# Attention scores in separate buffers, logits written straight into a group's rows, state update moved, fills moved ahead

## The chip, the cores and the metric

The kernel runs on one core of one Trainium2 chip. The metric is the device time of one execution in microseconds (us); the value before is the median of three runs. The engines are called by the profile's names: PE (matrix multiply; PEld is its weight load), DVE (vector), ACT (scalar), POOL (GpSimd) and SP, whose queue issues most of the transfers.

## The reference

The input is a gated linear attention with batch 4, 8 heads, 768 steps and head size 48, then a mixture of experts with 8 experts on the 3072 resulting rows of 384 numbers. All is float32.

```python
for t in range(S):
    state = alpha[:, :, t, :, None] * state + k[t] (outer) v[t]
    y[:, :, t] = q[t] @ state
x = y.transpose(0, 2, 1, 3).reshape(B * S, H * D)
logits = normalised(x) @ normalised(expert_emb).T / tau
expert_idx = argmax(logits, axis=1)
for e in range(E):                      # each token goes to one expert
    h = maximum(x[mask] @ w1[e], 0.0)   # 384 -> 1024
    out[mask] = gate_w[mask, None] * (h @ w2[e])
```

## The kernel before

The first stage computes attention and routing, the second (from L705 on) the experts. The sequence is cut into chunks of 128 steps: 6 per batch, 24 in all. The loop at L640 runs over an iteration number s and is a software pipeline. Iteration s does, in the order of the program text: `load(s + 2)`; `keys_back(s - 1)`, which turns the scaled keys on PE and copies them (ACT, `kb`); `rows(s - 3)`; `decays(s)`, which turns alpha, keys and queries on PE, runs two scans on DVE (`r` L458, `a` L472) and scales keys (DVE, `kr`) and queries (ACT copy `qc`, POOL product `qs`, L477); `decay_state(s - 1)` (POOL); `scores(s - 1)`; `update(s - 1)`; `mix_states(s - 2)` and `mix_chunk(s - 2)`; then the routing steps. Every third iteration `choose(g)` picks experts for a group of chunks on DVE (L310 to L317), and the iteration after it `place(g)` computes the rows in `xs` to which `to_rows` sends the tokens by indirect transfers from POOL. GROUPS (L61) has ten groups: six of three chunks, two of two, two of one.

The steps around the change, in the order of a chunk's life:

- `scores` multiplies keys and queries into one accumulator tile `sc` with two halves (even and odd heads). DVE masks half 0 into half 0 of the tile `sm` (L541); ACT copies half 1 into half 1 of the same tile (L544), and POOL clears the part above the diagonal (L545). `sm` has two buffers, `sc` one.
- `update` multiplies kept keys and values into `pd` (16 matmuls, L517), and DVE adds the result to the decayed state (L527), which POOL decays in the next iteration (`dec`, L502).
- `mix_states` (16 matmuls, L565) and `mix_chunk` (16 matmuls, L578) fill the accumulator `pyx`, which has one buffer; ACT copies its first part to `yT` (L584).
- one iteration later `rows` multiplies `yT` with a selection matrix `sel` (8 matmuls, L594) into the rest of `pyx`. DVE sums the two halves of the logits (`lg`, L603), ACT copies them into the token's row `x` (L607), two more ACT copies (L609) bring the 384 numbers, and a POOL copy (L601) the token's number. `x` has six buffers, one chunk each.

The matrix `sel` and the padded expert matrix `embp` are filled by POOL in `prepare_logits` (L270, L278, L285, L286: two fills and eight copies), which is put behind the scaled queries of chunk 1 by `behind(1)`.

Each engine runs its own queue in order and waits on semaphores. The program is written for a framework that places the waits and whose planner sets the order within each queue: it follows the program text, but by its own estimate of when operands are ready, so that some steps are interleaved (the turns of alpha for the next chunk stand partly ahead of the matmuls of `rows`). `behind(s)` forces what is inside it behind DVE's scan `a` and POOL's product `qs` of chunk s on these queues.

Of the kernel before, what the change touches and what calls it, by code (L numbers as in the profile page):

```python
# [27 lines left out]
def kernel(  # L28
# [155 lines left out]
    with ExitStack() as c1:  # L184
# [20 lines left out]
        def fixed_parts():  # L205
# [21 lines left out]

        sel = keep.tile([P, 2, NP // 2, 2 * D + E], FP32, name="sel")
        group_of = [g for g, (a, b) in enumerate(GROUPS) for _ in range(a, b)]
        lg_g = [  # L230
            keep.tile([P, b - a, E], FP32, name=f"lg{g}") for g, (a, b) in enumerate(GROUPS)
        ]

        al0 = keep.tile([P, NP, NS], FP32, name="al0")

        emb = work.tile([E, DM], FP32, name="emb", bufs=1)

        def prepare_loads():
            a0 = work.tile([NS, H, DP], FP32, name="a0", bufs=1)
            nc.vector.memset(a0[:, :, D:DP], 1.0)  # L240
            for b in range(B):
                nc.scalar.dma_start(
                    out=a0[b * NCH : (b + 1) * NCH, :, 0:D], in_=a_r[b, :, 0]
                )
            nc.scalar.dma_start(out=emb, in_=expert_emb)
            nc.scalar.dma_start(out=rtau, in_=tau.to_broadcast([P, 1]))
            return a0
# [11 lines left out]
        def prepare_logits():  # L259

            nc.vector.reciprocal(rtau, rtau)
            e2 = work.tile([E, DM], FP32, name="e2", bufs=1)
            en = work.tile([E, 1], FP32, name="en", bufs=1)
            nc.scalar.activation(e2, emb, AF.Square, accum_out=en)
            nc.scalar.activation(en, en, AF.Sqrt)
            nc.vector.tensor_scalar(en, en, 1e-6, None, ALU.add)
            nc.vector.reciprocal(en, en)
            nc.vector.tensor_tensor(en, en, rtau[:E], ALU.mult)
            embp = work.tile([E, 2, NP // 2, 2, DP], FP32, name="embp", bufs=1)
            nc.gpsimd.memset(embp, 0.0)  # L270
            for hh in range(2):
                nc.vector.tensor_scalar(
                    embp[:, hh, :, :, 0:D],
                    emb.rearrange("e (q j a d) -> e a q j d", q=NP // 2, j=2, a=2)[:, hh],
                    en, None, ALU.mult,
                )
            pe = ps_tr.tile([P, 2, NP // 2, E], FP32, tag="tr", name="pe")
            nc.gpsimd.memset(sel, 0.0)  # L278
            for hh in range(2):
                for q in range(NP // 2):  # L280
                    nc.tensor.transpose(
                        pe[:, hh, q],
                        embp[:, hh, q].rearrange("e j d -> e (j d)"), ident[:E, :E],
                    )
                    nc.gpsimd.tensor_copy(sel[0:DP, hh, q, 0:D], ident[0:DP, 0:D])  # L285
                    nc.gpsimd.tensor_copy(  # L286
                        sel[DP:P, hh, q, D : 2 * D], ident[DP:P, DP : DP + D]
                    )
            nc.vector.tensor_copy(sel[:, :, :, 2 * D :], pe)

# [12 lines left out]
        def choose(g):  # L303

            s0, s1 = GROUPS[g]
            n = s1 - s0
            shp = [P, n, E]
            l = lg_g[g][:, 0:n]
            top = work.tile([P, GMAX], FP32, name="top")[:, 0:n]
            nc.vector.tensor_reduce(top.unsqueeze(2), l, axis=AX.X, op=ALU.max)  # L310
            win = work.tile([P, GMAX, E], FP32, name="win")[:, 0:n]
            nc.vector.tensor_tensor(win, l, bc(top, shp, 2), ALU.is_equal)
            nc.vector.tensor_tensor(win, win, bc(first, shp, 1), ALU.mult)
            best = work.tile([P, GMAX], FP32, name="best")[:, 0:n]
            nc.vector.tensor_reduce(best.unsqueeze(2), win, axis=AX.X, op=ALU.max)
            ch = chosen[:, s0:s1]
            nc.vector.tensor_tensor(ch, win, bc(best, shp, 2), ALU.is_equal)  # L317
            for s in range(s0, s1):
                eng = nc.vector if s == NS - 1 else nc.gpsimd
                eng.tensor_tensor(before[:, s + 1], before[:, s], chosen[:, s], ALU.add)  # L320
# [103 lines left out]
        def load(s):  # L424

            if s < NS:
                b, c = divmod(s, NCH)
                i = s % NBUF
                for p0, p1 in ((1, AROW), (AROW, P)):
                    nc.sync.dma_start(out=at_s[i][p0:p1, :, 0:D], in_=a_r[b, c, p0:p1])  # L430
                nc.sync.dma_start(out=kt_s[i][:, :, 0:D], in_=k_r[b, c])
                nc.sync.dma_start(out=qt_s[i][:, :, 0:D], in_=q_r[b, c])
            if s > 0:
                b, c = divmod(s - 1, NCH)
                nc.sync.dma_start(out=vt_s[(s - 1) % NBV][:, :, 0:D], in_=v_r[b, c])
# [93 lines left out]
        def scores(s):  # L529

            d = st[s]
            kr, qs = d["kr"], d["qs"]
            d["sm"] = sm = work.tile([P, 2, NP, P], FP32, name="sm")
            sc = ps_sc.tile([P, 2, NP, P], FP32, name="sc")
            for p in range(NP):
                for hh in range(2):
                    sl = slice(DP * hh, DP * hh + DP)
                    nc.tensor.matmul(  # L538
                        sc[:, hh, p], lhsT=kr[sl, p], rhs=qs[sl, p], start=True, stop=True
                    )  # L540
            nc.vector.tensor_tensor(  # L541
                sm[:, 0], sc[:, 0], causal.to_broadcast([P, NP, P]), ALU.mult
            )
            nc.scalar.copy(sm[:, 1], sc[:, 1])  # L544
            nc.gpsimd.affine_select(  # L545
                out=sm[:, 1], in_=sm[:, 1], pattern=[[0, NP], [1, P]], base=0,
                channel_multiplier=-1, compare_op=ALU.is_ge, fill=0.0,
            )

# [21 lines left out]
        def mix_chunk(s):  # L571

            d = st[s]
            pyx, sm, vt = d["pyx"], d["sm"], vt_s[s % NBV]
            for hh in range(2):
                for p in range(NP):
                    q, to = p // 2, DP * (p % 2)
                    nc.tensor.matmul(  # L578
                        pyx[to : to + DP, hh, q * P : (q + 1) * P],
                        lhsT=vt[:, 2 * p + hh], rhs=sm[:, hh, p],  # L580
                        start=("dec" not in d and q == 0), stop=True, skip_group_check=True,
                    )
            d["yT"] = yT = work.tile([P, 2, NQ, P], FP32, name="yT")
            nc.scalar.copy(yT.rearrange("p a q t -> p a (q t)"), pyx[:, :, 0:YX])  # L584

        def rows(s):

            yT = st[s]["yT"]
            px = st[s]["pyx"][:, :, YX : YX + NQ * (2 * D + E)].rearrange(
                "t a (q n) -> t a q n", q=NQ  # L590
            )
            for hh in range(2):
                for q in range(NQ):
                    nc.tensor.matmul(  # L594
                        px[:, hh, q], lhsT=yT[:, hh, q], rhs=sel[:, hh, q], start=True, stop=True,
                        skip_group_check=True,
                    )
            g = group_of[s]
            s0, s1 = GROUPS[g]
            st[s]["x"] = x = work.tile([P, ROW], FP32, name="x", bufs=6)  # L600
            nc.gpsimd.tensor_copy(x[:, TK : TK + 1], toks[:, s : s + 1])  # L601
            l = lg_g[g][:, s - s0]
            nc.vector.tensor_reduce(  # L603
                l.unsqueeze(2), px[:, :, :, 2 * D :].rearrange("t a q e -> t e a q"),
                axis=AX.XY, op=ALU.add,
            )
            nc.scalar.copy(x[:, LG : LG + E], l)  # L607
            for hh in range(2):
                nc.scalar.copy(  # L609
                    x[:, 0:DM].rearrange("t (q j a d) -> t a q j d", q=NQ, j=2, a=2)[:, hh],  # L610
                    px[:, hh, :, 0 : 2 * D].rearrange("t q (j d) -> t q j d", j=2),
                )

        exg = xg_s[NXG - 1]
        exT = work.tile([P, KT, EARLY * P], FP32, name="exT", bufs=1)
# [20 lines left out]
        fixed_parts()  # L636
        load(0)
        a0 = prepare_loads()
        load(1)
        for s in range(NS + 4):  # L640
            if s + 2 <= NS:
# [10 lines left out]
            if 0 <= s - 1 < NS:  # L652
                decay_state(s - 1)
                scores(s - 1)
                update(s - 1)
            if 0 <= s - 2 < NS:
                mix_states(s - 2)
                mix_chunk(s - 2)
            if s == 1:
                with behind(s):  # L660
# [22 lines left out]
                        first_expert()  # L683
            with behind(s) if s < NS else ExitStack():
                for c in send[:] if s >= S0 + 3 else send[:1]:
                    to_rows(dest[:, c : c + 1], st[c]["x"])
                    send.remove(c)
            if r == S0 - 1:
                fetch_early()
# [259 lines left out]
```

## Time and profile before

| | |
|---|---|
| time, median of 3 runs (lowest to highest) | 480.54 us (479.85 to 486.49) |
| profiled execution | 481.05 us, its span 479.3 us |
| mean granted PE clock, share of full speed | 0.994 |
| PE busy | 444.9 us, 93% of the span |
| DVE, ACT, POOL busy | 176.3, 150.3, 139.3 us |
| attention stage | to about 173 us; the experts' stage fills the rest |

The span goes from the first to the last instruction of the profiled execution. Busy shares are averages over two stages with different limits, so they are read by stretch. The chain that ended last covers only the final part of the span here, and is not used.

### The profile page before, as it was taken

The page shows a single profiled execution, that of the slowest core. Times are in us where ns is not written, and L with a number is a line of the kernel's source. Part 1 is how long each engine was busy: PE and PEld are TensorE (multiplying, and loading weights), DVE is VectorE, ACT ScalarE, POOL GpSimd, SP SyncE. Part 2 cuts the span into 40 slices and gives each one's busy share as a digit, 9 for nine tenths or more (in the row PEclk, how much of TensorE's full clock was granted, in tenths as well). Part 3 has the DMA queues.
Part 4 walks back from the last instruction along what each step waited for, and adds up shares of the span by engine and source line. Part 5 has one row for each costly group of instructions (what it writes and reads, how often), then busy time and mean ns, then how long its engine had stood idle before and what let it go on. Part 6 is the DMA issues. An engine that isn't in the chain of part 4 may idle for free. (4 is left out here: it accounts for less than half of the span.)

```text
span 479.3 us, 8450 instructions
## 1 busy us (share of the span) xinstructions
PE 444.9 (93%) x3124; PEld 315.1 (66%) x3125; DVE 176.3 (37%) x467; ACT 150.3 (31%) x352; POOL 139.3 (29%) x236
## 2 busy tenths in 40 slices
PE   5798979888897999999999999999999999999993
PEld 4587868778786788577555555557557555655551
DVE  6777575776858751441211111111211121111010
ACT  3234434334343443463530421202540250210200
POOL 4546655655654742610001011010200101002001
PEclk9999989999999999999999999999999999999998
DMA  9999976876871396395503606301800900001000
GB/s 143 158 165 159 182 143 130 138 155 127 168 133 53 108 356 235 105 327 185 209 18 115 239 18 220 125 34 25 306 30 16 326 6 35 15 0 46 1 16 31
DMA packets 119358, 59.96 MB, mean 125 GB/s; under 512 B 102287, under 2 KB 113816, under 8 KB 119312
## 3 DMA queue, kind: packets, MB, share of 16 engines
q1 hardware_dynamic: 115208, 49.14, 44.4%
q0 software_dynamic: 3728, 10.16, 5.9%
q8 instruction: 28, 0.46, 0.4%
q14 instruction: 18, 0.15, 0.1%
q10 hardware_dynamic: 376, 0.05, 0.1%
HBM read 49.69 MB, written 11.45 MB: 128 GB/s over the span
## 5 line engine op out<-in xcount | busy, mean ns | idle before, releaser
L783 PE MATMUL ph<-xT,w 128*128 128x384 f32 (+1 forms) x384 | 119.6, 462 | 1.7 <-ACT hT L787 0.7
L794 PE MATMUL pyo<-w,hT 128*128 128x384 f32 x352 | 115.6, 488 | 0.0
L783 PEld LDWEIGHTS ph<-xT,w 128*128 128x128 f32 x384 | 67.6, 190 | 44.6 <-issue 5.2
L794 PEld LDWEIGHTS pyo<-w,hT 128*128 128x128 f32 x352 | 66.3, 190 | 45.3
L721 POOL DMA_INDIRECT out_dram<-y,sx x25 | 24.2, 967 | 239.6 <-DVE y L797 169.5
L787 ACT ACTIVATE hT<-ph 128x384 f32<-128x384 f32 (+1 forms) x64 | 28.6, 460 | 114.2 <-PE ph L783 114.1
L797 DVE TENSOR_SCALAR y<-pyo,gt 128x384 f32<-128x384 f32 x22 | 13.6, 617 | 114.1 <-PE pyo L794 114.1
L594 PE MATMUL pyx<-sel,yT 128*128 128x104 f32 x192 | 26.7, 282 | 15.7 <-ACT yT L584 15.3
L477 POOL TENSOR_TENSOR qs<-qc,a 128x512 f32<-128x512 f32 x24 | 30.5, 1271 | 26.0 <-DVE a L472 16.0
L594 PEld LDWEIGHTS pyx<-sel,yT 128*128 128x128 f32 x192 | 23.3, 191 | 19.4 <-ACT yT L584 19.2
L544 ACT COPY sm<-sc 128x512 f32<-128x512 f32 x24 | 14.1, 587 | 61.1 <-DVE sm L541 61.1
L458 DVE TENSOR_TENSOR_SCAN r<-pa,inr 128x511 f32<-128x511 f32 x24 | 29.2, 1218 | 4.5 <-PE pa L414 4.1
L292 POOL DMA_INDIRECT xs<-x,dest x24 | 24.6, 1024 | 19.3 <-DVE dest L341 11.7
L472 DVE TENSOR_TENSOR_SCAN a<-pa,ini 128x512 f32<-128x512 f32 x24 | 29.4, 1223 | 0.9
L538 PE MATMUL sc<-qs,kr 64*128 64x128 f32 x384 | 29.6, 291 | 0.1
L578 PE MATMUL pyx<-sm,vt 128*64 128x128 f32 x384 | 26.3, 278 | 2.1 <-DVE sm L541 2.1
L538 PEld LDWEIGHTS sc<-qs,kr 64*128 64x128 f32 x384 | 24.6, 192 | 4.5 <-issue 2.9
L737 DVE COPY xT<-pxg 128x384 f32<-128x384 f32 (+1 forms) x30 | 14.7, 498 | 30.3 <-PE pxg L736 27.3
L578 PEld LDWEIGHTS pyx<-sm,vt 128*64 128x64 f32 x384 | 20.5, 136 | 5.6 <-issue 3.4
L414 PE MATMUL pa<-ident,at 128*128 128x128 f32 x96 | 18.3, 287 | 4.3 <-DMA at<-in_alpha_dram 4.3
L746 ACT ACTIVATE gx<-xg 128x384 f32<-128x384 f32 x32 | 16.7, 522 | 14.5 <-DMA xg<-xs 13.3
L476 ACT COPY qc<-pq 128x512 f32<-128x512 f32 x24 | 14.1, 586 | 11.5 <-PE pq L414 10.7
(168 smaller groups left out, 524.6 us busy)
## 6 DMA issues: line engine op xcount, KB each, us to landing
w<-in_moe_w_dram SPq DMA_DIRECT2D x16, 1536.0 KB, 8.0
kt<-in_k_dram SPq DMA_DIRECT2D x24, 192.0 KB, 3.9
qt<-in_q_dram SPq DMA_DIRECT2D x24, 192.0 KB, 4.5
vt<-in_v_dram SPq DMA_DIRECT2D x24, 192.0 KB, 4.0
xg<-xs SPq DMA_DIRECT2D x22, 196.5 KB, 7.6
at<-in_alpha_dram SPq DMA_DIRECT2D x24, 168.0 KB, 3.9
xg<-xs SPq DMA_DIRECT2D x8, 98.2 KB
at<-in_alpha_dram SPq DMA_DIRECT2D x24, 22.5 KB, 4.1
```

Source lines behind the costliest of these rows:

```text
L292: ins = nc.gpsimd.indirect_dma_start(out=xs, out_offset=bass.IndirectOffsetOnAxis(ap=rows, axis=0), in_=x, in_offset=None, bounds_check=E ...
L414: nc.tensor.transpose(pt[:, p * P : (p + 1) * P], t[:, 2 * p : 2 * p + 2].rearrange("p h d -> p (h d)"), ident,)
L458: nc.vector.tensor_tensor_scan(r[:, L - 2 :: -1], pa[:, L - 1 : 0 : -1], inr[:, L - 2 :: -1], 1.0, ALU.mult, ALU.add,)
L472: by_dve = nc.vector.tensor_tensor_scan(a, pa, ini, 0.0, ALU.mult, ALU.add)
L477: by_pool = nc.gpsimd.tensor_tensor(qs.rearrange("p n t -> p (n t)"), qc, a, ALU.mult)
L538: nc.tensor.matmul(sc[:, hh, p], lhsT=kr[sl, p], rhs=qs[sl, p], start=True, stop=True)
L578: nc.tensor.matmul(pyx[to : to + DP, hh, q * P : (q + 1) * P], lhsT=vt[:, 2 * p + hh], rhs=sm[:, hh, p], start=("dec" not in d and q == 0) ...
L594: nc.tensor.matmul(px[:, hh, q], lhsT=yT[:, hh, q], rhs=sel[:, hh, q], start=True, stop=True, skip_group_check=True,)
L721: ins = nc.gpsimd.indirect_dma_start(out=out, out_offset=bass.IndirectOffsetOnAxis(ap=col, axis=0), in_=y, in_offset=None, bounds_check=N - 1,
L783: nc.tensor.matmul(ph, lhsT=w1_t[:, i, f * P : (f + 1) * P], rhs=xT[:, i], start=(i == 0), stop=(i == KT - 1),)
L787: nc.scalar.activation(hT[:, f], ph, AF.Relu)
L794: nc.tensor.matmul(py, lhsT=hT[:, f], rhs=w2_t[:, f], start=(f == 0), stop=(f == FT - 1),)
```

## The change

The two halves of `sc` and of `sm` become two tiles each, of half the size. The logits are summed straight into the rows of a group's buffer `x` (one tile for up to three chunks, three buffers), out of which `choose` reads them and `to_rows` sends; the logits' own tiles `lg` and ACT's copy of them go away, ACT's two copies of the 384 numbers become one, and the token numbers are copied once per group and not once per chunk. `update` is called between `mix_states` and `mix_chunk`. The ten POOL fills for `embp` and `sel` are called ahead of `load(1)`, and so ahead of the queries of chunk 0.

```diff
+        def prepare_fills():
+            nc.gpsimd.memset(embp, 0.0)
+            nc.gpsimd.memset(sel, 0.0)
+            for hh in range(2):
+                for q in range(NP // 2):
+                    nc.gpsimd.tensor_copy(sel[0:DP, hh, q, 0:D], ident[0:DP, 0:D])
+                    nc.gpsimd.tensor_copy(
+                        sel[DP:P, hh, q, D : 2 * D], ident[DP:P, DP : DP + D]
+                    )
...
-            l = lg_g[g][:, 0:n]
+            l = x_g[g][:, :, LG : LG + E]
...
-            d["sm"] = sm = work.tile([P, 2, NP, P], FP32, name="sm")
-            sc = ps_sc.tile([P, 2, NP, P], FP32, name="sc")
+            d["sm"] = sm = [work.tile([P, NP, P], FP32, name=f"sm{hh}") for hh in range(2)]
+            sc = [ps_sc.tile([P, NP, P], FP32, name=f"sc{hh}") for hh in range(2)]
...
-            nc.vector.tensor_tensor(
-                sm[:, 0], sc[:, 0], causal.to_broadcast([P, NP, P]), ALU.mult
-            )
-            nc.scalar.copy(sm[:, 1], sc[:, 1])
+            nc.vector.tensor_tensor(sm[0], sc[0], causal.to_broadcast([P, NP, P]), ALU.mult)
+            nc.scalar.copy(sm[1], sc[1])
...
-            st[s]["x"] = x = work.tile([P, ROW], FP32, name="x", bufs=6)
-            nc.gpsimd.tensor_copy(x[:, TK : TK + 1], toks[:, s : s + 1])
-            l = lg_g[g][:, s - s0]
+            if s == s0:
+                x_g[g] = work.tile([P, GMAX, ROW], FP32, name="x", bufs=3)[:, 0 : s1 - s0]
+                nc.gpsimd.tensor_copy(x_g[g][:, :, TK], toks[:, s0:s1])
+            x = x_g[g][:, s - s0]
             nc.vector.tensor_reduce(
-                l.unsqueeze(2), px[:, :, :, 2 * D :].rearrange("t a q e -> t e a q"),
+                x[:, LG : LG + E].unsqueeze(2), px[:, :, :, 2 * D :].rearrange("t a q e -> t e a q"),
                 axis=AX.XY, op=ALU.add,
             )
-            nc.scalar.copy(x[:, LG : LG + E], l)
-            for hh in range(2):
-                nc.scalar.copy(
-                    x[:, 0:DM].rearrange("t (q j a d) -> t a q j d", q=NQ, j=2, a=2)[:, hh],
-                    px[:, hh, :, 0 : 2 * D].rearrange("t q (j d) -> t q j d", j=2),
-                )
+            nc.scalar.copy(
+                x[:, 0:DM].rearrange("t (q j a d) -> t a q j d", q=NQ, j=2, a=2),
+                px[:, :, :, 0 : 2 * D].rearrange("t a q (j d) -> t a q j d", j=2),
+            )
...
         a0 = prepare_loads()
+        prepare_fills()
         load(1)
...
                 scores(s - 1)
+            if 0 <= s - 2 < NS:
+                mix_states(s - 2)
+            if 0 <= s - 1 < NS:
                 update(s - 1)
             if 0 <= s - 2 < NS:
-                mix_states(s - 2)
                 mix_chunk(s - 2)
```

## Rows read from the trace of the kernel before

**Rows 1.** Busy time of the engines, share of span and instructions, from the page.

```profile
PE 444.9 (93%) x3124; PEld 315.1 (66%) x3125; DVE 176.3 (37%) x467; ACT 150.3 (31%) x352; POOL 139.3 (29%) x236
```

**Rows 2.** Windows: length, busy us by engine (instructions), clock, DMA share, GB/s.

```profile
18.85:173.20 154.35, 137.07 (x1832) 118.26 (x1832) 111.32 (x225) 61.51 (x148) 89.06 (x158) 0.99 0.79 145
25.63:59.00 33.37, 30.58 (x422) 26.07 (x420) 23.14 (x45) 13.94 (x34) 19.60 (x33) 1.00 1.16 167
67.23:75.35 8.12, 8.12 (x94) 7.26 (x93) 4.98 (x11) 3.11 (x8) 3.96 (x8) 0.80 0.56 99
87.52:129.22 41.70, 36.88 (x500) 31.91 (x500) 29.88 (x58) 17.00 (x42) 23.55 (x41) 1.00 0.77 144
110.28:117.06 6.78, 6.62 (x94) 5.85 (x93) 5.24 (x12) 3.02 (x8) 3.36 (x6) 1.00 0.66 118
300.00:400.00 100.00, 99.55 (x402) 62.70 (x401) 15.41 (x51) 27.75 (x63) 10.60 (x11) 1.00 0.30 104
```

**Rows 3.** Waits: engine, line, releaser: us in total, times, longest.

```profile
ACT sm L544 <- DVE sm L541: 61.1, 24, 4.2
...
ACT x L607 <- DVE lg L603: 22.0, 21, 2.6
POOL x L601 <- DMA xs<-x,dest: 21.4, 13, 2.8
...
PE pyx L594 <- ACT yT L584: 15.3, 12, 2.6
```

**Rows 4.** Timeline, one iteration with `choose`: start, us, engine, line [idle before <-releaser].

```profile
102.25 1.22 DVE L458 TENSOR_TENSOR_SCAN r<-pa,inr 128x511 f32<-128x511 f32 x1
102.31 0.64 POOL L545 TENSOR_SCALAR_AFFINE_SELECT sm<-sm 128x512 f32<-128x512 f32 x1
...
103.02 1.16 PE L538 MATMUL sc<-qs,kr 64*128 64x128 f32 x16
...
104.46 1.23 DVE L472 TENSOR_TENSOR_SCAN a<-pa,ini 128x512 f32<-128x512 f32 x1
...
104.62 1.04 PE L578 MATMUL pyx<-sm,vt 128*64 128x128 f32 x16
...
105.83 1.26 POOL L477 TENSOR_TENSOR qs<-qc,a 128x512 f32<-128x512 f32 x1
...
106.03 1.10 DVE L317 TENSOR_TENSOR chosen<-win,best 128x24 f32<-128x24 f32 x1
...
107.05 0.68 DVE L541 TENSOR_TENSOR sm<-sc,causal 128x512 f32<-128x512 f32 x1
...
107.65 0.41 DVE L527 TENSOR_TENSOR state<-pd,dec 128x256 f32<-128x256 f32 x1
107.76 0.59 ACT L544 COPY sm<-sc 128x512 f32<-128x512 f32 x1 [4.00 <-DVE sm L541]
108.24 0.59 ACT L584 COPY yT<-pyx 128x512 f32<-128x512 f32 x1
...
108.89 1.14 PE L594 MATMUL pyx<-sel,yT 128*128 128x104 f32 x8 [2.42 <-ACT yT L584]
...
110.13 0.19 DVE L603 TENSOR_REDUCE lg<-pyx 128x8 f32<-128x32 f32 x1 [2.07 <-PE pyx L594]
```

**Rows 5.** Timeline, the iteration after it: end of `mix_chunk`, and its copy.

```profile
113.35 1.09 PE L578 MATMUL pyx<-sm,vt 128*64 128x128 f32 x16
...
114.74 0.59 ACT L584 COPY yT<-pyx 128x512 f32<-128x512 f32 x1
```

**Rows 6.** Timeline of the start: POOL's queries and fills, and chunk 2's first scan.

```profile
8.94 1.27 POOL L477 TENSOR_TENSOR qs<-qc,a 128x512 f32<-128x512 f32 x1 [4.16 <-DVE al L257]
...
15.55 0.51 POOL L270 MEMSET embp<- 8x512 f32 x1
...
18.34 0.22 POOL L286 COPY sel<-ident 64x48 f32<-64x48 f32 x1
...
18.85 1.22 DVE L458 TENSOR_TENSOR_SCAN r<-pa,inr 128x511 f32<-128x511 f32 x1 [0.76 <-PE pa L414]
```

More of the change, by code (lines that the diff above doesn't have):

```diff
@@ L229 @@
         group_of = [g for g, (a, b) in enumerate(GROUPS) for _ in range(a, b)]
-        lg_g = [
-            keep.tile([P, b - a, E], FP32, name=f"lg{g}") for g, (a, b) in enumerate(GROUPS)
-        ]
+        x_g = {}
         al0 = keep.tile([P, NP, NS], FP32, name="al0")
         emb = work.tile([E, DM], FP32, name="emb", bufs=1)
+        embp = work.tile([E, 2, NP // 2, 2, DP], FP32, name="embp", bufs=1)
+        def prepare_fills():
[7 more added lines that the diff above has]
+                    )
         def prepare_loads():
@@ L268, in prepare_logits @@
             nc.vector.tensor_tensor(en, en, rtau[:E], ALU.mult)
-            embp = work.tile([E, 2, NP // 2, 2, DP], FP32, name="embp", bufs=1)
-            nc.gpsimd.memset(embp, 0.0)
             for hh in range(2):
@@ L277, in prepare_logits @@
             pe = ps_tr.tile([P, 2, NP // 2, E], FP32, tag="tr", name="pe")
-            nc.gpsimd.memset(sel, 0.0)
             for hh in range(2):
@@ L283, in prepare_logits @@
                         embp[:, hh, q].rearrange("e j d -> e (j d)"), ident[:E, :E],
-                    )
-                    nc.gpsimd.tensor_copy(sel[0:DP, hh, q, 0:D], ident[0:DP, 0:D])
-                    nc.gpsimd.tensor_copy(
-                        sel[DP:P, hh, q, D : 2 * D], ident[DP:P, DP : DP + D]
                     )
@@ L538, in scores @@
                     nc.tensor.matmul(
-                        sc[:, hh, p], lhsT=kr[sl, p], rhs=qs[sl, p], start=True, stop=True
+                        sc[hh][:, p], lhsT=kr[sl, p], rhs=qs[sl, p], start=True, stop=True
                     )
-            nc.vector.tensor_tensor(
-                sm[:, 0], sc[:, 0], causal.to_broadcast([P, NP, P]), ALU.mult
-            )
-            nc.scalar.copy(sm[:, 1], sc[:, 1])
+            nc.vector.tensor_tensor(sm[0], sc[0], causal.to_broadcast([P, NP, P]), ALU.mult)
+            nc.scalar.copy(sm[1], sc[1])
             nc.gpsimd.affine_select(
-                out=sm[:, 1], in_=sm[:, 1], pattern=[[0, NP], [1, P]], base=0,
+                out=sm[1], in_=sm[1], pattern=[[0, NP], [1, P]], base=0,
                 channel_multiplier=-1, compare_op=ALU.is_ge, fill=0.0,
@@ L579, in mix_chunk @@
                         pyx[to : to + DP, hh, q * P : (q + 1) * P],
-                        lhsT=vt[:, 2 * p + hh], rhs=sm[:, hh, p],
+                        lhsT=vt[:, 2 * p + hh], rhs=sm[hh][:, p],
                         start=("dec" not in d and q == 0), stop=True, skip_group_check=True,
@@ L599, in rows @@
             s0, s1 = GROUPS[g]
-            st[s]["x"] = x = work.tile([P, ROW], FP32, name="x", bufs=6)
-            nc.gpsimd.tensor_copy(x[:, TK : TK + 1], toks[:, s : s + 1])
-            l = lg_g[g][:, s - s0]
+            if s == s0:
+                x_g[g] = work.tile([P, GMAX, ROW], FP32, name="x", bufs=3)[:, 0 : s1 - s0]
+                nc.gpsimd.tensor_copy(x_g[g][:, :, TK], toks[:, s0:s1])
+            x = x_g[g][:, s - s0]
             nc.vector.tensor_reduce(
-                l.unsqueeze(2), px[:, :, :, 2 * D :].rearrange("t a q e -> t e a q"),
+                x[:, LG : LG + E].unsqueeze(2), px[:, :, :, 2 * D :].rearrange("t a q e -> t e a q"),
                 axis=AX.XY, op=ALU.add,
             )
-            nc.scalar.copy(x[:, LG : LG + E], l)
-            for hh in range(2):
-                nc.scalar.copy(
-                    x[:, 0:DM].rearrange("t (q j a d) -> t a q j d", q=NQ, j=2, a=2)[:, hh],
-                    px[:, hh, :, 0 : 2 * D].rearrange("t q (j d) -> t q j d", j=2),
-                )
+            nc.scalar.copy(
+                x[:, 0:DM].rearrange("t (q j a d) -> t a q j d", q=NQ, j=2, a=2),
+                px[:, :, :, 0 : 2 * D].rearrange("t a q (j d) -> t a q j d", j=2),
+            )
         exg = xg_s[NXG - 1]
@@ L685 @@
                 for c in send[:] if s >= S0 + 3 else send[:1]:
-                    to_rows(dest[:, c : c + 1], st[c]["x"])
+                    to_rows(dest[:, c : c + 1], x_g[group_of[c]][:, c - GROUPS[group_of[c]][0]])
                     send.remove(c)
```

## The prediction

> **What bounds the kernel now.** Read first the page's busy times: PE is busy for 444.9 us, no other engine for 40% of the span [rows 1]. That is an average, so the windows come next. In the experts' stage PE is busy for 99.55 of 100 us: nothing that another engine does there can be felt, and what the attention stage gains reaches the end whole. In the attention stage, from chunk 2 to the drain, PE is busy for 137.07 of 154.35 us, so 17.3 us are pauses [rows 2]. A repeating pattern is six chunks: 41.70 us, PE 36.88, DVE 29.88, ACT 17.00, POOL 23.55. No engine is full; a chain between them sets the pace.
>
> The waits name it: PE stood still before `rows` twelve times, 15.3 us in all, for ACT's copy `yT`; and ACT stood still before its copy of score half 1 in all 24 chunks, 61.1 us, for DVE's mask of half 0 [rows 3]. The copy uses nothing of what the mask writes. Look at the order in one iteration: the scores end at 104.18; DVE is busy with the scan and with `choose`, and masks half 0 only at 107.05 to 107.73; ACT, idle for 4.00 us, starts its copy 0.03 after that; `yT` stands behind it in ACT's queue although `mix_chunk` was over at 105.66; PE starts `rows` at 108.89 after a pause of 2.42; and DVE, idle for 2.07, can then sum logits and start the next chunk [rows 4]. So it is a ring: DVE's mask, ACT, ACT, PE, DVE. Its length, not the work, sets the long iterations.
>
> **Score halves in own buffers.** ACT's copy then needs only the scores. In that iteration it runs at about 104.3 to 104.9, while ACT idles. `yT` waits for `mix_chunk` alone: in the next iteration the time from the end of `mix_chunk` (113.35 + 1.09 = 114.44) to `yT` (114.74) is 0.30 [rows 5], so `yT` runs from 105.96 to 106.55 and `rows` starts 0.06 later (as 108.24 + 0.59 to 108.89), at 106.6 instead of 108.89. Of a pause of 2.42, 0.14 is left. Twelve waits keep 12 x 0.14 = 1.7 of 15.3: **13.6 us** gained. The bounds are 0 (ACT stays late) and 15.3.
>
> What is late next is DVE: in an iteration with `choose` it works without a gap from 102.25 to the end of the state at 108.06, then sums logits; its next scan comes 0.15 after that starts, as now (110.13 to 110.28, where this iteration ends [rows 2, 4]). That gives 108.06 + 0.19 + 0.15 = 108.4, a gain of 1.9 for this iteration and not 2.3. Three iterations have a pause of this size, so **-1.2 us**; bounds 0 and -2.
>
> POOL's clearing of half 1 (0.64) moves with the copy. Now it runs beside the scan `r`, which takes its usual 1.22 [rows 4]; at about 104.95 to 105.6 it would run beside the scan `a` and be over before POOL's `qs` at 105.83. I take no cost. What a collision costs is seen at `chosen`: it takes 1.10 and ends when `qs` ends. The Trainium skill, "SBUF — State Buffer", section "Who interferes with whom", says that a vector instruction with two inputs in SBUF contends with a GpSimd instruction that reads SBUF, and that one with a single SBUF input doesn't; both rows agree. Read against this change, the rule makes a later clearing costly; that is a rival below.
>
> **Logits into the group's rows.** 24 ACT copies of the logits and their wait (22.0 us [rows 3]) go, two copies become one, 24 POOL copies become 10. All of this lies on ACT and POOL, busy for 17.00 and 23.55 of 41.70 us, beside PE: 0 on the path. The accumulator `pyx` comes free earlier, which `mix_states`, now 16 matmuls earlier in PE's queue, can use. The reads of `choose` become strided, with as many elements: 0. The sends keep their number and place.
>
> **Update behind the state part.** 16 matmuls change places with 16 others on PE; the sum is the same. DVE's add of the state waits for them, and nothing but the next iteration's work is queued behind it: it now starts at 107.65, behind the mask, over three microseconds after the scores, and the matmuls end some 0.7 later than before. POOL's `dec` behind it is used an iteration later: 0. If DVE were less late, the add would be the next to wait, for at most these 0.7.
>
> **Fills ahead of the queries.** Ten POOL instructions, no transfers, about 3.0 us (15.55 to 18.56), leave the place behind chunk 1's queries and pass the queries of chunks 0 and 1 on POOL's queue. They fall into POOL's idle 4.16 us before 8.94 [rows 6]; were that cover gone, chunk 0's queries would be 3.0 late. SP's loads wait for none of them. Freed is the first `dec` and the clearing of chunk 0, which stood behind the fills. The gain lies between 0 (PE's own order sets the start) and 3.0; I take the idle time of DVE before chunk 2's scan, **0.8 us**, the nearest row.
>
> **The clock.** The window from 67.23 ran at a mean granted clock of 0.80, a mixture of 2.4 and 1.2 GHz, right after the longest of the twelve waits (2.6). It took 8.12 us for 94 PE instructions; the window from 110.28 took 6.78 for 94 at 1.00 [rows 2]. Without the pause before it I expect the full clock: **1.3 us**; bounds 0 and 1.3.
>
> **Sum.** 13.6 - 1.2 + 0.8 + 1.3 = 14.5. The profiled execution took 481.05, with 1.75 outside its span, and becomes 466.5. It lies 0.5 above the median of the runs, so 466.0 us.
>
> **The rivals.**
>
> *No effect:* the tie between mask and copy isn't the common buffer but an order that stays, for instance ACT's copy being placed behind other work. For it: the profile names a wait, not its reason. Against: 24 of 24 starts follow the mask, and the two share nothing but the tiles. Only the start's 0.8 remains: 479.7.
>
> *The clearing collides:* POOL does it late, behind `qs`, and DVE's steps of `choose` with two SBUF inputs wait up to 0.64 more. Seven or eight iterations have `choose`; 7 x 0.64 = 4.5: 470.5. For it: `chosen` is already held. Against: the scores are ready before the scan ends. It is worked out from the rows alone; the rule named above is why it is listed.
>
> *Transfers become the bound:* the same bytes (144 GB/s over 41.70 us) in 36.88 us need 163 GB/s. For it: the DMA share is already 0.77. Against: 167 GB/s were moved from 25.63 to 59.00, and PE waited for no load there [rows 2]. If only 150 hold, six chunks take 144/150 x 41.70 = 40.0, which gains 1.7 per pattern, 6 us over the stage, and 8 with the start and the clock: 472.5.
>
> *Slower, the group's buffer:* the POOL copy of the token numbers opens a group's buffer and waits until the sends of the group three before have landed; `qs` and the clearing queue behind it, and the DVE sum and ACT copy of the rows need that buffer too. Now 13 of 24 such copies wait, 21.4 us in all, 2.8 at the longest [rows 3], though there are six buffers. Seven of ten groups reuse a buffer: 7 x 2.8 = 19.6 on the path would give 466 + 19.6 = 485.6. It decides if the last send of the old group comes less than that wait before the new group's first row. Against: by the program these are three iterations apart, some 18 us, and today's waits overlap with POOL's wait for the scan.
>
> **How the numbers follow.** Chances: forecast 0.62 (its own range 462 to 470), no effect 0.12, collision 0.10, transfers 0.08, slower 0.06, other 0.02. With every pause, the clock and all fills gained it would be 480.5 - 17.3 - 1.3 - 3.0 = 459; I give less than 461 little. The range 461 to 476 takes in the forecast, the collision and the transfers, and leaves out no effect and slower: about 0.2. Two per cent, which is about what a measurement of this kernel can tell from no change, is 9.6 us: faster means below 470.9. The forecast, over half of the collision and a little of the rest give 0.68; of the slower case only its upper part exceeds 2%: 0.03; the rest, 0.29, is within.
>
> **What would show it.** Right: ACT's copy of half 1 starts within 0.3 us of the scores' end; the wait of PE's `rows` for `yT` falls from 15.3 to about 2; no iteration takes over 7 us; six chunks take 37 to 38.5. The clock stays at 1.00 around 60 to 70. The first scan of chunk 2 comes before 18.85. Wrong: `rows` waits as long for `yT`, now behind another ACT step; `chosen` or the steps before it take much longer; PE waits for loads; POOL's copy of token numbers shows long waits with `qs` late behind it. The forecast fails if PE's freed pauses turn up before `scores` or the turns instead.

## The result and the profile after

| | before | after |
|---|---|---|
| median of the runs | 480.31 us | 463.75 us |
| profiled execution, its span | 481.05, 479.3 us | 463.7, 461.9 us |

The ratio of the runs is 0.963, 95% interval 0.956 to 0.969: faster, and 2.2 us below the predicted 466.0, inside the range. The busy times of the page, and PE's granted clock in 40 slices of the span (tenths of full speed):

```profile
PE 440.5 (95%) x3124; PEld 312.7 (68%) x3125; DVE 173.2 (38%) x467; ACT 146.7 (32%) x304; POOL 136.8 (30%) x222
...
PEclk9999999999999999999999999999999999999997
```

and the clock's slices before:

```profile
PEclk9999989999999999999999999999999999999998
```

PE does the same work in a span that is 17.4 us shorter, and the dent of the clock in the attention stage is gone; only the last slice is lower, as it was. The windows (length, busy us of PE, PEld, DVE, ACT, POOL with instructions, clock, DMA share, GB/s) that answer to [rows 2]: the stage from chunk 2 on, the iteration with 94 PE instructions, a pattern of six chunks, and one iteration of it.

```profile
18.50:154.00 135.50, 130.35 (x1816) 113.70 (x1814) 106.63 (x222) 58.53 (x106) 83.36 (x138) 1.00 0.87 159
...
61.17:68.02 6.85, 6.44 (x94) 5.77 (x93) 5.10 (x12) 2.86 (x6) 5.12 (x11) 1.00 1.14 196
74.17:111.34 37.17, 36.00 (x502) 31.57 (x501) 28.77 (x58) 16.18 (x29) 22.72 (x37) 1.00 0.88 167
105.19:111.34 6.15, 6.15 (x90) 5.34 (x89) 4.29 (x7) 2.79 (x5) 3.33 (x5) 1.00 0.78 159
```

Six chunks take 37.17 us instead of 41.70, and PE stands still for 1.17 us in them instead of 4.82. In the last window it has no pause at all. The waits (engine, line, releaser: us in total, times, longest) against [rows 3]:

```profile
ACT x L608 <- DVE x L604: 19.5, 19, 3.0
...
POOL x L602 <- DMA xs<-x,dest: 11.6, 5, 5.2
...
ACT sm L544 <- PE sc L540: 10.3, 16, 2.0
...
PEld pyx L565 <- ACT x L608: 4.1, 5, 1.0
...
PE pyx L565 <- ACT x L608: 3.1, 4, 0.8
...
PEld pyx L594 <- ACT yT L584: 2.7, 14, 0.5
```

ACT's copy of half 1 now waits for the scores and for nothing of DVE's. PE's wait for `yT` has left the matmuls' list but for 0.2 us; what is left is on the weight loads, 2.7 us, mostly 0.17 or 0.18 at a place, where the matmuls show no pause. PE's wait in `mix_states` for ACT's copy of the rows has grown, from 1.2 to 3.1 us. An iteration with `choose`, to be read against [rows 4]:

```profile
92.79 1.22 DVE L460 TENSOR_TENSOR_SCAN r<-pa,inr 128x511 f32<-128x511 f32 x1
...
93.56 1.16 PE L540 MATMUL sc<-qs,kr 64*128 64x128 f32 x16
...
94.85 0.58 ACT L544 COPY sm<-sc 128x512 f32<-128x512 f32 x1 [0.54 <-PE sc L540]
...
96.31 0.59 ACT L584 COPY yT<-pyx 128x512 f32<-128x512 f32 x1 [0.88 <-PE pyx L578]
...
96.36 1.28 POOL L479 TENSOR_TENSOR qs<-qc,a 128x512 f32<-128x512 f32 x1 [2.07 <-DVE win L315]
96.42 0.68 DVE L543 TENSOR_TENSOR sm<-sc,causal 128x512 f32<-128x512 f32 x1
...
96.95 1.14 PE L594 MATMUL pyx<-sel,yT 128*128 128x104 f32 x8
97.02 0.66 DVE L319 TENSOR_TENSOR chosen<-win,best 128x24 f32<-128x24 f32 x1
...
98.19 0.19 DVE L604 TENSOR_REDUCE x<-pyx 128x8 f32<-128x32 f32 x1 [0.17 <-issue]
...
98.35 1.22 DVE L460 TENSOR_TENSOR_SCAN r<-pa,inr 128x511 f32<-128x511 f32 x1
...
98.82 0.64 POOL L545 TENSOR_SCALAR_AFFINE_SELECT sm<-sm 128x512 f32<-128x512 f32 x1
```

The scores end at 94.72, ACT copies at 94.85, `yT` is ready at 96.90 and PE goes on at 96.95 without a pause. The next scan starts 5.56 us after the last; it was 8.03. Two things stand elsewhere than the prediction had them: DVE's mask runs ahead of the last step of `choose`, not behind it, and POOL's clearing still comes late, at 98.82.

### The profile page after: what moved, and what is told of

It reads as the page before. It is cut to its first block, busy times and chain, and to the rows that moved or that the text cites. A ratio compares the mean times of both kernels' runs of the same rounds, so it can differ in the third digit from the quotient of the medians.

```text
span 461.9 us, 8401 instructions
## 1 busy us (share of the span) xinstructions
PE 440.5 (95%) x3124; PEld 312.7 (68%) x3125; DVE 173.2 (38%) x467; ACT 146.7 (32%) x304; POOL 136.8 (30%) x222
## 5 line engine op out<-in xcount | busy, mean ns | idle before, releaser
L790 ACT ACTIVATE hT<-ph 128x384 f32<-128x384 f32 (+1 forms) x64 | 28.6, 460 | 114.2 <-PE ph L786 114.1
L800 DVE TENSOR_SCALAR y<-pyo,gt 128x384 f32<-128x384 f32 x22 | 13.6, 618 | 114.1 <-PE pyo L797 114.1
L584 ACT COPY yT<-pyx 128x512 f32<-128x512 f32 x24 | 14.1, 586 | 31.5 <-PE pyx L578 31.5
L608 ACT COPY x<-pyx 128x384 f32<-128x384 f32 x24 | 11.6, 484 | 23.8 <-DVE x L604 19.5
```

Source lines behind the costliest of these rows:

```text
L790: nc.scalar.activation(hT[:, f], ph, AF.Relu)
```

## The experiments

Each ratio compares a kernel with the kernel before, both run on the same chip; times are medians. The experiments ran on three chips, so that times of kernels from different ones are less comparable than ratios.

**Both halves, nothing else.** The kernel before with this edit alone:

```diff
-            d["sm"] = sm = work.tile([P, 2, NP, P], FP32, name="sm")
-            sc = ps_sc.tile([P, 2, NP, P], FP32, name="sc")
+            d["sm"] = sm = [work.tile([P, NP, P], FP32, name=f"sm{hh}") for hh in range(2)]
+            sc = [ps_sc.tile([P, NP, P], FP32, name=f"sc{hh}") for hh in range(2)]
```

> The kernel before with the score halves in tiles of their own (both the accumulators sc and the masked tiles sm) and nothing else changed. Ring theory: the tie between DVE's mask and ACT's copy is nearly all of the gain: 465 to 468 us, PE's wait before the rows' matmuls for yT falls from 15.3 us to under 2. Rival (relief theory: the gain comes from the ACT and POOL copies that go and from the fills): 474 or more.

Measured 466.11 us, ratio 0.969 (0.961 to 0.978). PE's wait for `yT` is gone from its list. The ring is most of the gain; the relief theory falls.

**Which of the two tiles.** The accumulator `sc` alone, then the masked scores `sm` alone:

> The kernel before with only the accumulator sc split into two tiles; the masked scores stay in one tile sm. If the tie is in the accumulator: as with both split, 465 to 468 us, ACT's copy no longer waits for DVE. If the tie is in sm: no change, 480 us, ACT's copy waits some 61 us for DVE.

> The kernel before with only the masked scores sm split into two tiles; the accumulator sc stays one tile. If the tie is in the accumulator: no change, 479 to 481 us, and ACT's copy still waits some 61 us for DVE's mask. If it is in sm: 465 to 468.

Measured 466.29 us (ratio 0.970, 0.961 to 0.979) for `sc` alone, and 481.85 (1.002, 0.997 to 1.007) for `sm` alone. The waits with `sm` split:

```profile
ACT sm L544 <- DVE sm L541: 61.8, 24, 4.1
...
PE pyx L594 <- ACT yT L584: 15.1, 15, 2.6
```

and with `sc` split:

```profile
ACT sm L544 <- PE sc L538: 10.7, 17, 1.6
...
PE pyx L565 <- ACT x L609: 3.1, 5, 1.0
```

The tie is in the accumulator. Two engines that only read its two halves were put one behind the other; splitting `sm`, which both engines write, does nothing. With `sc` split, the two reads can overlap in time:

```profile
84.57 0.68 DVE L541 TENSOR_TENSOR sm<-sc,causal 128x512 f32<-128x512 f32 x1
84.75 0.59 ACT L544 COPY sm<-sc 128x512 f32<-128x512 f32 x1
```

**The order of the text.** All tiles as before, the two instructions exchanged:

```diff
+            nc.scalar.copy(sm[:, 1], sc[:, 1])
             nc.vector.tensor_tensor(
                 sm[:, 0], sc[:, 0], causal.to_broadcast([P, NP, P]), ALU.mult
             )
-            nc.scalar.copy(sm[:, 1], sc[:, 1])
```

> The kernel before with the two instructions exchanged in the program text: ACT's copy of half 1 ahead of DVE's mask of half 0, all tiles as before. Ring theory: the tie turns round, the mask now waits for ACT's copy, which is early, so yT is no longer late: 465 to 469 us. If any common tile is enough to keep the ring: 478 to 481.

Measured 466.56 us, ratio 0.971 (0.963 to 0.980). The waits:

```profile
ACT sm L541 <- PE sc L538: 10.0, 18, 1.4
...
DVE sm L542 <- ACT sm L541: 2.5, 4, 0.7
```

The tie has turned round, and costs almost nothing that way: the later reader in the text waits for the earlier, and ACT is early. One exchanged line brings what the split brings.

**The rest without the halves.** The changed kernel with `sc` and `sm` joined again (the first diff, backwards).

> The changed kernel with sc and sm each in one tile again: the change without the halves. Ring theory: the ring is back, 477 to 481 us, PE's rows wait some 14 us for yT. Relief theory (fewer ACT and POOL copies, earlier fills): 466 to 470.

Measured 485.88 us, ratio 1.014 (1.008 to 1.020): the ring is back, but the time is above what was expected, 5 us over the kernel before (480.5 on this chip). The waits, and windows of seven iterations:

```profile
ACT sm L546 <- DVE sm L543: 62.7, 23, 4.0
...
PE pyx L596 <- ACT yT L586: 17.0, 15, 2.4
```

```profile
60.84:69.57 8.73, 6.31 (x74) 5.62 (x73) 5.86 (x13) 2.77 (x6) 5.49 (x12) 0.91 0.75 141
69.57:76.88 7.31, 7.31 (x94) 6.51 (x93) 4.95 (x11) 2.73 (x6) 3.57 (x5) 0.88 0.59 110
89.05:96.98 7.93, 6.95 (x84) 6.25 (x85) 4.71 (x11) 3.66 (x8) 4.98 (x10) 1.00 0.96 152
103.91:111.94 8.03, 5.62 (x74) 4.92 (x73) 5.83 (x13) 2.63 (x5) 4.95 (x10) 1.00 0.82 150
111.94:118.72 6.78, 6.47 (x94) 5.76 (x93) 5.24 (x11) 2.76 (x6) 3.37 (x6) 1.00 0.67 118
130.88:140.33 9.45, 8.48 (x84) 7.59 (x85) 4.71 (x12) 3.68 (x8) 5.07 (x10) 0.82 0.77 128
146.89:156.03 9.14, 6.72 (x74) 6.03 (x73) 5.86 (x13) 2.78 (x6) 5.09 (x11) 0.85 0.24 67
```

PE waits 17.0 us for `yT`, 1.7 more than before. What is above the kernel before is the clock: in four of these windows it is at 0.82 to 0.91, and iterations of the same kind (the same number of PE instructions) at 1.00 show what that costs. 9.45 us stand against 7.93, and so do 9.35 at a further place (44.92 to 54.27, at 0.82); 8.73 + 7.31 stand against 8.03 + 6.78, and 9.14 against 8.03. Together these are 5.3 us, where the profile of the kernel before has one such place and lost 1.3 [rows 2]. The difference, 4.0, is no less than the 3.7 us between the two spans (483.0 and 479.3). So in these profiles the other edits without the halves show no gain or loss that is clear of the clock. Why the clock falls more often in this kernel was not tried.

**The three other edits, each put back in the changed kernel.** First kernel: the fills behind chunk 1's queries. Second: `update` ahead of `mix_states`. Third: a row buffer for each chunk, with the logits' own tiles and the copies as before.

```diff
-        prepare_fills()
         load(1)
...
-            if 0 <= s - 2 < NS:
-                mix_states(s - 2)
             if 0 <= s - 1 < NS:
                 update(s - 1)
             if 0 <= s - 2 < NS:
+                mix_states(s - 2)
                 mix_chunk(s - 2)
...
+            st[s]["x"] = x = work.tile([P, ROW], FP32, name="x", bufs=6)
+            l = lg_g[g][:, s - s0]
```

> The changed kernel with the ten POOL fills put back to where the expert matrix is prepared, behind chunk 1's queries. By the prediction's step they are worth 0.8 us (bounds 0 and 3): 464.5 us; by the two traces, in which chunk 2's first scan moved only from 18.85 to 18.50: 0.4 or less.

> The changed kernel with the state update back ahead of the state part. By the prediction 0: 463.7 us. If the earlier state part is what makes PE wait for ACT's copy of the rows (3.1 us after the change, 1.2 before), going back gains up to 2 us: 462.

> The changed kernel with the logits in tiles of their own, a row buffer for each chunk, three ACT copies and one POOL copy for each chunk, as before. By the prediction 0: 463 to 465 us. If the shorter path from the rows' matmuls to the free accumulator pyx counts, now that PE has few pauses: up to 24 x 0.3 = 7 us slower, 470.

Measured 464.06 us (runs 463.4 to 465.8), 464.26 (463.8 to 465.1) and 465.30 (464.8 to 466.2), where the changed kernel took 463.2 to 464.3 in ten runs, none of them beside these three. The fills and the update are worth about half a microsecond at most, which is within the spread. With the update back PE waits 2.0 instead of 3.1 us for ACT's copy of the rows, yet the time doesn't fall. The rows are worth some 1.5 us, far less than the 7 of the rival, and by another path than the rival's. With the rows put back:

```profile
74.37 0.18 POOL L603 COPY x<-toks 128x1 f32<-128x1 f32 x1 [2.91 <-DMA xs<-x,dest]
74.51 1.27 POOL L481 TENSOR_TENSOR qs<-qc,a 128x512 f32<-128x512 f32 x1
...
75.84 1.16 PE L542 MATMUL sc<-qs,kr 64*128 64x128 f32 x16 [0.59 <-POOL qs L481]
```

POOL's copy of a token's number, now once per chunk, waits for sends that have not landed (28.6 us at 15 places, against 11.6 at five); `qs` stands behind it, and PE's scores wait for `qs`, 2.1 us at three places. The changed kernel has no such wait in its matmuls' list.

**What is late next.** In the changed kernel `choose` was called ahead of `scores`, and the mask forced behind its last step, where it stood before:

```diff
+                    picked = choose(g)
...
+                if picked is not None:
+                    queue.enter_context(tc.issue_after(picked.ins))
                 nc.vector.tensor_tensor(sm[0], sc[0], causal.to_broadcast([P, NP, P]), ALU.mult)
```

> The changed kernel with choose called ahead of the scores and DVE's mask forced behind the last step of choose on DVE's queue, the order of the kernel before. In the changed kernel the mask (0.68) runs while POOL's qs holds up that last step, which then takes 0.66 instead of 1.1. If DVE is what is late next, as the prediction had it (-1.2 us for three iterations), this order costs 1.2 to 3 us: 465 to 467. If DVE has slack in these iterations: within 0.5 us of the changed kernel.

> The changed kernel once more, on the chip of the two others, to compare with them: 463.7 us.

Measured 465.98 us (465.1 to 466.6) against 463.70 (463.2 to 463.9) for the changed kernel on the same chip: 2.3 us. The timeline:

```profile
97.68 1.27 POOL L480 TENSOR_TENSOR qs<-qc,a 128x512 f32<-128x512 f32 x1 [2.07 <-DVE win L315]
...
97.86 1.13 DVE L319 TENSOR_TENSOR chosen<-win,best 128x24 f32<-128x24 f32 x1
...
98.91 0.68 DVE L547 TENSOR_TENSOR sm<-sc,causal 128x512 f32<-128x512 f32 x1
...
99.94 1.20 DVE L461 TENSOR_TENSOR_SCAN r<-pa,inr 128x511 f32<-128x511 f32 x1
```

`chosen` starts beside POOL's `qs`, takes 1.13 us and ends when that ends; mask, state and next scan come behind it. In the changed kernel the mask fills this time and `chosen` takes 0.66. PE feels it in `mix_states`, which waits 4.9 us instead of 3.1 for ACT's copy of the rows, itself behind DVE's sum. So DVE is the next to be late. The 2.3 us are the price of the edit as a whole, the earlier call of `choose` and the forced order.

**The same tie at another place.** DVE's sum of the logits and ACT's copy of the rows both read `pyx`; the copy waits for the sum. The two were exchanged in the text:

```diff
-            nc.vector.tensor_reduce(
-                x[:, LG : LG + E].unsqueeze(2), px[:, :, :, 2 * D :].rearrange("t a q e -> t e a q"),
-                axis=AX.XY, op=ALU.add,
-            )
             nc.scalar.copy(
                 x[:, 0:DM].rearrange("t (q j a d) -> t a q j d", q=NQ, j=2, a=2),
                 px[:, :, :, 0 : 2 * D].rearrange("t a q (j d) -> t a q j d", j=2),
             )
+            nc.vector.tensor_reduce(
+                x[:, LG : LG + E].unsqueeze(2), px[:, :, :, 2 * D :].rearrange("t a q e -> t e a q"),
+                axis=AX.XY, op=ALU.add,
+            )
```

> The changed kernel with ACT's copy of a chunk's 384 numbers ahead of DVE's sum of its logits in the program text. Both read the accumulator pyx, and ACT's copy now waits for DVE's sum (17.5 us in all). If readers of one accumulator tile wait for each other in the order of the text, as with the scores, the wait turns round: PE's wait for this copy falls from 3.1 us to under 1.5, and the time to 461.5 to 463. Rival: DVE's sum, later by the copy's 0.48, holds up the scan behind it: 464 to 468.

Measured 462.00 us (461.4 to 462.4), ratio 0.959 (0.954 to 0.963): 1.7 us faster than the changed kernel on the same chip, and the slowest of its six runs is faster than the fastest of that kernel's six. The long iteration of the pattern in the changed kernel, and in this one:

```profile
79.25 1.20 DVE L460 TENSOR_TENSOR_SCAN r<-pa,inr 128x511 f32<-128x511 f32 x1
...
81.84 0.17 DVE L604 TENSOR_REDUCE x<-pyx 128x8 f32<-128x32 f32 x1
...
82.04 0.48 ACT L608 COPY x<-pyx 128x384 f32<-128x384 f32 x1 [0.65 <-DVE x L604]
...
82.57 0.67 PE L565 MATMUL pyx<-qs,dec 64*64 64x128 f32 x16 [0.76 <-ACT x L608]
...
86.64 1.22 DVE L460 TENSOR_TENSOR_SCAN r<-pa,inr 128x511 f32<-128x511 f32 x1
```

```profile
79.46 1.20 DVE L460 TENSOR_TENSOR_SCAN r<-pa,inr 128x511 f32<-128x511 f32 x1
...
80.30 0.48 ACT L604 COPY x<-pyx 128x384 f32<-128x384 f32 x1 [1.23 <-PE pyx L594]
...
82.06 0.17 DVE L608 TENSOR_REDUCE x<-pyx 128x8 f32<-128x32 f32 x1
...
82.28 0.67 PE L565 MATMUL pyx<-qs,dec 64*64 64x128 f32 x16 [0.27 <-DVE x L608]
...
86.35 1.22 DVE L460 TENSOR_TENSOR_SCAN r<-pa,inr 128x511 f32<-128x511 f32 x1 [0.83 <-PE pa L416]
```

The copy no longer waits until DVE, behind its scan, sums the logits; PE's pause before `mix_states` falls from 0.76 to 0.27 and the iteration from 7.39 to 6.89 us. It occurs once in six chunks, three times in all. PE's wait in all fell from 3.1 to 2.2, not to under 1.5 as expected: at one place near the start it grew, from 0.80 to 1.39, because the sum that `mix_states` now waits for comes late there. This version beats both kernels.

## Why the prediction was right

*The ring.* Shown: it carries most of the gain. Half 1's copy alone freed from the mask gives 466.3 us, the whole change 463.75. In the profiles, the time from chunk 2's first scan to chunk 23's is 147.54 us before, 132.52 with `sc` alone split and 131.00 after. The prediction left open which of the tiles made the tie and named both; it is `sc` alone. The Trainium skill, "PSUM — Partial Sum Buffer", section "PSUM bank collisions raise a hardware error", says that two engines must not access one bank at once in the same partitions, reads included, and gives a bank 512 fp32 values in each partition, which is the 128x512 of one half. By that the halves needn't wait for each other if each fills a bank of its own. No row shows where the halves lie; the runs agree so far as the two reads overlap once the tiles are separate (84.57 to 85.25 and 84.75 to 85.34 above), and as one tile wait for each other in the order of the text.

*The size of the stall, too small by 3.* The term 13.6 was made from the matmuls' wait of 15.3, with 0.14 left in each of twelve places. In the same list the weight loads of these matmuls waited longer:

```profile
PEld pyx L594 <- ACT yT L584: 19.2, 15, 2.8
```

This is what went down to 2.7, so 16.5 us were regained. The ends of matmuls are modelled in the profile, and the first part of a pause, in which the last matmul is still shown as busy, is missing from the matmuls' row: at three of the fifteen places (37.20 us is one) the weight loads waited 0.37 and the matmuls show no pause at all. In the iteration of the timeline above nothing is left: the turns of keys and alpha last until `yT` is there.

*What is late next, -1.2: did not come.* DVE is late next, as the forced order shows, but the planner put the mask ahead of `chosen` in every kernel with `sc` split in which it was free to. (Where only the two instructions were exchanged it left the mask behind.) The chip's part in it: `chosen` reads two SBUF tiles and is held until `qs` ends, while the mask, with one input from the accumulator, ran its usual 0.68 beside `qs`. The Trainium skill, "SBUF — State Buffer", section "Who interferes with whom", says just this of instructions with two and with one input in SBUF, and both rows agree.

*The clock, 1.3: came.* The iteration with 94 PE instructions takes 6.85 us at 1.00 instead of 8.12 at 0.80. It is a term of this one execution: equal pauses stay at 1.00 elsewhere in it, and with `sm` alone split, the ring whole, ten runs went from 477.31 us at a mean clock of 0.998 to 483.77 at 0.987.

*The start, 0.8: too large.* Chunk 2's first scan:

```profile
18.50 1.22 DVE L460 TENSOR_TENSOR_SCAN r<-pa,inr 128x511 f32<-128x511 f32 x1 [0.76 <-PE pa L416]
```

0.35 us earlier. The idle time before it is still 0.76, as in [rows 6]; the row that I took as nearest measured something else, PE's order. The fills' own worth is 0.3 by the run with them put back (464.06, the scan at 18.77), within the spread.

*Costed at nothing.* Opening the ring brought a pause that was not foreseen: `mix_states` waits for ACT's copy of the rows, on the weight loads 4.1 us instead of 2.2. It isn't the edits of rows and update that bring it, for it is 4.0 with `sc` alone split. The rows edit, put at 0 on the path, is worth some 1.5 us once the ring is open. PE's scores then wait for `qs` behind POOL's copy of the token's number, 1.4 us with `sc` alone split, and the edit takes this away; the prediction saw this path only as a danger of the new buffer.

*The sum.* From chunk 2's first scan to chunk 23's the time fell from 147.54 to 131.00 us, 16.5 less. The terms give 16.5 + 1.3 - 1.9 = 15.9; 0.6 is not assigned. With 0.35 at the start and 0.5 in the tail this is the span's 17.4. The predicted gain was 14.5, so it lies as near as it does in part by luck: the stall was 2.9 too small and 1.2 was taken off for DVE in vain, while 1.9 for the rows' copy was left out and the start was 0.45 too large.

*The rivals.* No effect is refuted by the split of `sc`, and would have been true had only `sm` been split. Transfers: 167 GB/s in the pattern, more than the 163 worked out, and PE waited for no load in it. The group's buffer: POOL waited 11.6 us at five places instead of 21.4 at thirteen, though up to 5.2 at one, and the time fell. The collision: the clearing stayed where it was, beside the scan `r`, so this rival was not tested; neither was my placing of it right. One sign was wrong: four iterations still take 7.4 to 7.5 us, each next to one of 4.5 to 5.1. Three of them are the long one of the pattern, with PE's pause of 0.76 before `mix_states`; it is the six chunks that count.

## What to carry to other kernels

If an engine starts work at the very end of another's instruction, time after time, and the two only share a tile that both read, exchange them in the text or split the tile before anything else: the reader that is early must not stand behind the one that is late. Size a pause of PE by the weight loads' wait, not by the matmuls' alone, and take off what stays where PE has no pause (here some 0.17 us at a place). When a ring is opened, look at the queue order of the engine that is late next; it was worth more here than any of the three side edits.

## What was not expected of the hardware

A pause can cost twice, but not every one does. In the kernel before and in the changed kernel with `sc` and `sm` joined again, the granted clock fell in or right after iterations in which PE had paused for 1.8 to 2.6 us, to a mixture of its levels of 2.4 and 1.2 GHz (0.80 to 0.95 over an iteration), at 1.1 to 1.5 us a place: one place before, four with the halves joined. Other pauses of these lengths stayed at 1.00 in the same profiles: that of 2.42 in [rows 4], and those in the windows from 89.05 (1.81) and 103.91 (2.42). In the profile of the changed kernel no iteration from the first scan to chunk 23's fell. Near the start the clock also fell without the ring: to 0.90 with both halves alone split (10.98 to 19.65) and to 0.90 and 0.87 with the two instructions exchanged (11.30 to 26.94). What decides was not found.
